# Maxima across partitions by a TensorE transpose, a VectorE maximum of the row and a one-row matmul, instead of a GpSimd reduction

## The chip, the core and the metric

The kernel runs on one core of a Trainium2 chip. The metric is the device time of one execution in microseconds (us). Engines are named as the profile names them: PE is the matmul engine (PEld its weight loads), DVE the vector engine, ACT the scalar engine, POOL GpSimd, SP the engine that issues the DMA transfers. Each engine executes its own instructions in program order, and a semaphore makes one wait for another. PSUM, where PE writes its results, is divided into banks of 2 KB in each partition; the kernel gives each result a bank of its own.

## What is computed

Banded attention over two batches of 768 tokens with eight heads, and behind it two layers of a mixture of experts over the 1536 tokens. All experts see all tokens.

```python
def _moe_ref(x, w_gate, w1, w2) -> np.ndarray:
    ...
    logits = x @ w_gate
    logits = logits - logits.max()
    P = np.exp(logits)
    for _ in range(8):
        P /= P.sum(1, keepdims=True) + 1e-09
        P /= P.sum(0, keepdims=True) + 1e-09
        P *= N / E
    out = np.zeros((N, D), dtype=np.float32)
    for e in range(E):
        h = np.maximum(x @ w1[e], 0.0)
        ye = h @ w2[e]
        out += P[:, e:e + 1] * ye
```

The first layer has eight experts; the second has four, and its weights P are given probabilities divided by their sum over the experts. `w1[e]` is 512 x 1024, `w2[e]` 1024 x 512.

## The kernel before

**Tiling.** The attention runs first (141 us of the profiled execution), then twelve experts one after the other (0 to 7 of the first layer, 8 to 11 of the second). An expert takes the tokens in three chunks of 512 (chunk 0, 1, 2). A chunk is a first product (`hidden`: 28 block products of six 128x256 matmuls each, L913, into PSUM tiles `ph`) and a second (`mixed`: 14 block products of twelve, L990, into `py`). Both are products of two by two blocks in seven instead of eight parts, and every operand is split into a high and a low float16 part, so that three matmuls make one. Between the block products DVE, ACT and POOL add blocks up (`c`, `s`), take the relu and split the results into parts (`hh` high, `hl` low) for the second product, and DVE adds `py` to the rows `acc` (L1112). A half of `hidden` covers half of the columns; its 14 block products come before those of the other half.

**Order.** The order of each engine's instructions is the order in which the program is written (`manual_schedule`). After each block product of `hidden` and each half block product of `mixed` the program calls `tick()`, which executes the small work that is due: 56 ticks a chunk, 168 an expert. The table `TICKS` says at which tick of an expert each piece of small work goes into the order; for most experts its entry "other" holds. `BALANCE` does the same for the steps of `sinkhorn` (the eight balancing iterations on `logits`, in expert 0), and `WAITS` for what follows a block product.

**The matrix scales.** Before a matrix is split into float16 parts, a power of two is found that brings its largest magnitude into range. During expert i this is done for both matrices of expert i + 1, and during the attention for expert 0: the pieces are loaded by DMA, DVE takes each piece's largest magnitude per partition (`wm`, L281) and the largest of the four (`wmm`, L290), POOL takes the largest over the 128 partitions (`wma`, L291), and DVE makes the power of two in three instructions (`pow2`, L254, L257, L259: `ws` and `wi`). In "other" the first matrix has its `wmm` and `wma` at tick 64 and `pow2` at 67, in chunk 1; the second at 120 and 123, in chunk 2. The operands of the first matrix are made from tick 111 on, those of the second in the next expert. There are 24 matrices, and `sinkhorn` has one more maximum over partitions (`mm`, L779).

**PSUM.** In the experts two pools of four banks serve all results: "ps" for those that are read only once and "pa" for the sums that several block products add to (`BANK` 0: the `ph` of products 1, 6, 7, 4, so two such tiles in each half of `hidden`), for `pt`, `pg` of the rows, and, by the same pools, for the `pc` of `sinkhorn`. A new tile takes the next bank of its pool, and PE waits until that bank's last reader is done.

Of the kernel before, what the change touches and what calls it, by code (L numbers as in the profile page):

```python
# [19 lines left out]
P = 128  # L20
GW = 32          # keys at the front that the banded attention covers as global ones
BW = P - GW      # keys before a query tile that it covers as local ones
BIG = 1.0e12
EXPONENT = 0x7F800000
# products of two by two blocks (Winograd's form of Strassen's scheme): operands of each
PRODUCTS = {1: (0, 0), 2: (1, 1), 3: (6, 2), 4: (2, 6), 5: (3, 3), 6: (4, 4), 7: (5, 5)}
BANK = {1: 0, 6: 0, 7: 0, 4: 0, 2: 1, 5: 2, 3: 2}
FIRST = (1, 2, 5)        # those that start a sum; the others add to one that has been read
ORDER1 = (1, 5, 6, 2, 7, 3, 4)
ORDER2 = (1, 5, 2, 6, 3, 7, 4)  # L30
# the quarter of the second product that a sum goes to, after each product
QUARTER = {5: (1, 1), 1: (0, 0), 6: (0, 1), 2: (0, 0), 7: (1, 1), 3: (0, 1), 4: (1, 0)}
PLACE2 = (0, 2, 3, 1, 4, 5, 6)   # where the second matrix's operands are
# the steps of the attention's even and odd units: what, and of which unit (how many before this one)
# [9 lines left out]
# The small work goes between the matrix products at numbers of ticks, counted from the start of an expert (28 for  # L44
# a chunk's product, 168 in all; during the attention: 2 a unit). Of an expert, by where it stands:
#   next1, next2: loads, largest magnitudes and scale of the next expert's first and second matrix
#   operands1: of its first matrix; for each half of the columns and each tile of the rows of a half the high and low
#     part of the first block, of the second row of blocks, the sums, the high and low part of two and of two sums
#   replace: the difference in place of its second matrix's second block
#   operands2: of its own second matrix; for each tile of the rows of a half the high and low part of the rows of  # L50
#     blocks, a sum and its parts, two sums and their parts
# "first": the first expert, -1: the last of the first layer, 0: the first of the second layer, "other": the others.
TICKS = {
    "attention": {
        "next1": ((2, 5, 7, 7), (11, 14, 13, 16), (18, 19)),
        "next2": ((11, 16, 40, 42), (22, 22, 43, 47), (49, 50)),
# [60 lines left out]
# the rows that become the second layer's operands in pairs of tiles: where the expert stands, the tile; ticks of the  # L117
# scales, the transposes, the sums, the high and low parts
# [8 lines left out]
# the same for the last rows of the attention, and their gate  # L127
KEPT = (36, 39, 44, 47, 49, 46, 48, 47, 49, 49, 50, 52, 54, 53, 55, 54, 56, 55, 60, 48, 51)
# the steps that balance the mixing weights
BALANCE = (58, 61, 58, 60, 62, 77, 80, 81, 82, 87, 87, 94, 97, 98, 98, 103, 104, 111, 114, 116, 118, 125, 122,  # L130
           143, 147, 149)
# the first expert's results: their weights, each row tile of a chunk
RESCALE = (5, 13, 14, 17, 18, 67, 79, 70, 72, 75, 121, 130, 121, 128, 127)
# ticks from a product to what follows from it, in each half of a hidden chunk
WAITS = ((0, 1, 0, 1, 0, 3, 1, 5, 3, 5, 0, 2, 7),
         (0, 1, 0, 1, 0, 1, 1, 5, 3, 5, 0, 3, 5))

# [1020 lines left out]
```

## Time and profile before

| | |
|---|---|
| times of three runs | 1735.85, 1732.91, 1747.15 us; median 1735.85 |
| the profiled execution, its span | 1735.8 us |
| busy: PE, DVE, POOL, ACT | 88 %, 76 %, 57 %, 55 % |
| mean granted TensorE clock | 0.94 of full speed |
| attention | 141 us |
| one chunk of expert 11, which prepares no next expert | 36.7 us |
| chunks 0, 1, 2 of expert 3 | 40.1, 43.1, 48.8 us |

The span of the profiled execution is the whole of its time to 0.1 us, and equals the median of the runs. A timeline row gives start and duration of an instruction, the engine, the line, output and inputs, and in brackets how long the engine had been idle before it and what released it. A row of the waits view reads: who waited for whom, total us, times, longest. Matmuls overlap: a 128x256 matmul is shown with 0.27 us, and one starts every 0.109 us at the full clock.

### The profile page before, as it was taken

Reading aid. Unit: us, or ns where it says so; the run is one execution under the profiler, and the core shown is the slowest. Engines: PE = TensorE matmul, PEld = TensorE weight load, DVE = VectorE, ACT = ScalarE, POOL = GpSimd, SP = SyncE. Lnnn points to the kernel's source line nnn. Section 1 sums busy time; section 2 is a strip of 40 time slices with the busy share of each in tenths; the row PEclk is TensorE's granted clock in tenths of the full one; section 3 lists DMA queues with packets and bytes.
Section 4 is the critical chain, followed back from the end, with each engine's and each line's share of the span. In section 5 each row is a group of like instructions: output and inputs, shape, how many; then the busy total and the mean of one; then the engine's idle time right before and its main releaser. Section 6 shows DMA issues by size and latency. Waiting matters only on the chain.

```text
span 1735.8 us, 35028 instructions
## 1 busy us (share of the span) xinstructions
PE 1532.3 (88%) x13216; PEld 1336.9 (77%) x13216; DVE 1311.4 (76%) x2903; ACT 954.7 (55%) x2515; POOL 988.2 (57%) x1274
## 2 busy tenths in 40 slices
PE   8999788888988998998998998988898898988998
PEld 7988677777877876886876886876777777777787
DVE  7897578769768757857857867877988857867855
ACT  6796536436546535535545545656665635635643
POOL 1466447448547538538537637566746735835833
PEclk9798989999998998998998999999999999999999
DMA  9520201101101101101101101100200200100011
GB/s 215 117 60 1 86 1 50 50 2 49 50 2 49 50 1 50 50 1 49 49 2 49 50 2 49 50 2 15 84 2 14 77 10 11 64 26 1 7 35 37
DMA packets 73972, 67.93 MB, mean 39 GB/s; under 512 B 52288, under 2 KB 55360, under 8 KB 73792
## 3 DMA queue, kind: packets, MB, share of 16 engines
q1 hardware_dynamic: 73792, 65.59, 13.1%
q8 instruction: 105, 1.72, 0.4%
q14 instruction: 75, 0.61, 0.1%
HBM read 62.43 MB, written 3.15 MB: 38 GB/s over the span
## 4 chain that ended last, share of the span: by engine, by line
PE 50%; POOL 21%; DVE 15%; ACT 7%; issue 7%; DMA 0%; POOLq 0%; DVEq 0%; SPq 0%; ACTq 0%
PE ph L913 27%; PE py L990 18%; POOL hl L903 14%; POOL st L305 6%; DVE w1l L298 4%; DVE w2l L298 2%; DVE acc L1112 2%; PE op L583 2%; ACT hh L903 2%; DVE s L893 1%; ACT w2h L297 1%; ACT c L945 1%; PE ep L567 1%; DVE c L893 1%; DVE xl L1051 1%
## 5 line engine op out<-in xcount | busy, mean ns | idle before, releaser
L913 PE MATMUL ph<-xh,w1h 128*128 128x256 f16 x2016 | 569.6, 283 | 110.3 <-ACT c L945 102.5
L903 POOL TENSOR_TENSOR hl<-c,hh 128x256 f16<-128x256 f32 x632 | 466.3, 765 | 246.1 <-issue 89.7
L990 PE MATMUL py<-w2h,hh 128*128 128x256 f16 x2016 | 555.1, 275 | 34.5 <-DVE acc L1112 26.6
L990 PE MATMUL py<-w2l,hh 128*128 128x256 f16 x2016 | 555.3, 275 | 26.5 <-DVE w2l L298 26.3
L913 PE MATMUL ph<-xl,w1h 128*128 128x256 f16 x2016 | 569.3, 282 | 0.0
L913 PE MATMUL ph<-xh,w1l 128*128 128x256 f16 x2016 | 568.3, 282 | 0.0
L990 PE MATMUL py<-w2h,hl 128*128 128x256 f16 x2016 | 555.5, 276 | 6.7 <-POOL hl L903 6.4
L913 PEld LDWEIGHTS <-w1h 128*128 128x128 f16 x4032 | 408.1, 101 | 176.0 <-issue 116.3
L990 PEld LDWEIGHTS <-hh 128*128 128x128 f16 x4032 | 398.3, 99 | 88.8 <-issue 39.6
L903 ACT ACTIVATE hh<-c 128x256 f16<-128x256 f32 x720 | 279.3, 416 | 117.6 <-DVE c L903 93.5
L945 ACT ACTIVATE c<-ph 128x256 f32<-128x256 f32 x432 | 158.1, 382 | 270.7 <-PE ph L913 245.7
L1112 DVE SCALAR_TENSOR_TENSOR acc<-py,mix,acc 128x256 f32<-128x256 f32 x438 | 204.5, 476 | 125.3 <-PE py L990 124.2
L990 PEld LDWEIGHTS <-hl 128*128 128x128 f16 x2016 | 199.0, 99 | 67.4 <-issue 23.4
L913 PEld LDWEIGHTS <-w1l 128*128 128x128 f16 x2016 | 204.3, 101 | 30.5
L291 POOL PARTITION_ALL_REDUCE wma<-wmm x24 | 9.1, 380 | 280.6 <-PE ph L913 140.6
L903 POOL TENSOR_TENSOR hl<-s,hh 128x256 f16<-128x256 f32 x144 | 117.4, 823 | 69.8 <-ACT hh L903 61.1
L903 DVE TENSOR_TENSOR c<-c,s 128x256 f32<-128x256 f32 x144 | 89.4, 621 | 83.0 <-POOL hl L903 83.0
L889 ACT ACTIVATE c<-c 128x256 f32<-128x256 f32 x288 | 117.3, 407 | 53.9 <-DVE c L948 45.5
L305 POOL TENSOR_TENSOR st<-raw 128x256 f32<-128x256 f32 x144 | 124.6, 875 | 16.6 <-issue 15.3
L305 POOL TENSOR_TENSOR st<-st,raw 128x256 f32<-128x256 f32 x144 | 125.3, 886 | 12.5 <-DVE w2l L298 8.7
L281 DVE TENSOR_REDUCE wm<-raw 128x1 f32<-128x1024 f32 x96 | 112.5, 1208 | 0.0
L298 DVE SCALAR_TENSOR_TENSOR w1l<-st,ws,w1h 128x512 f16<-128x512 f32 x96 | 97.4, 1014 | 15.3 <-ACT w1h L297 15.2
(157 smaller groups left out, 2000.0 us busy)
## 6 DMA issues: line engine op xcount, KB each, us to landing
raw<-in_moe_w_dram SPq DMA_DIRECT2D x96, 512.0 KB, 4.0
rows<-in_v_dram SPq DMA_DIRECT2D x12, 256.0 KB, 5.4
out_dram<-acc SPq DMA_DIRECT2D x24, 128.0 KB, 1.7
rows<-in_k_dram SPq DMA_DIRECT2D x11, 256.0 KB, 6.1
rows<-in_q_dram SPq DMA_DIRECT2D x10, 256.0 KB, 5.7
vA<-in_v_dram SPq DMA_DIRECT2D x10, 192.0 KB, 4.3
vA<-in_v_dram SPq DMA_DIRECT2D x10, 64.0 KB, 4.2
xh<-in_q_dram SPq DMA_DIRECT2D x2, 256.0 KB, 4.9
```

The lines of the kernel that those rows point to most:

```text
L281: nc.vector.tensor_reduce(out=wm[:, c:c + 1], in_=r, axis=AX.X if len(r.shape) == 2 else AX.XY, op=ALU.max, apply_absolute_value=True)
L297: return [lambda: nc.scalar.activation(hi(), src(), AF.Copy, scale=scale), lambda: nc.vector.scalar_tensor_tensor(out=lo(), in0=src(), sca ...
L298: lambda: nc.vector.scalar_tensor_tensor(out=lo(), in0=src(), scalar=scale, in1=hi(), op0=ALU.mult, op1=ALU.subtract)]
L305: nc.gpsimd.tensor_tensor(out=out, in0=a, in1=b, op=op)
L583: nc.tensor.matmul(op[:, h * D:(h + 1) * D], et[:, h, n, :], loaded[t, "v" + c][:, 4 * g + h, :], start=(n == 0), stop=(n == len(cs) - 1))
L889: nc.scalar.activation(out, src, AF.Relu)
L893: nc.vector.scalar_tensor_tensor(out=out, in0=src, scalar=0.0, in1=other, op0=ALU.max, op1=op)
L903: urgent.setdefault(state["tick"] + n, []).append(lambda: f(*args))
L913: nc.tensor.matmul(dst, a[:, wi, fs], b[:, r, :], start=(n in FIRST and m == 0), stop=(m == 3 * HC - 1), skip_group_check=n not in FIRST)
L945: nc.scalar.activation(c[p, n], src, AF.Copy)
L990: nc.tensor.matmul(src, a[:, ts], w[:, bi, :], start=(n in FIRST and k == 0), stop=(k == 3 * NH - 1), skip_group_check=n not in FIRST)
L1112: nc.vector.scalar_tensor_tensor(out=a, in0=pp, scalar=mx[:, o:o + 1], in1=a, op0=ALU.mult, op1=ALU.add)
```

## The change

Each maximum over partitions on POOL is replaced. PE transposes the column of 128 maxima into one row of PSUM (`mt`, after L290), DVE takes the maximum of that row (`top`, after L296), PE multiplies it by a row of ones, so that it stands on all 128 partitions in PSUM (`ma`, after L294), and `pow2` reads it there. A scale so has five steps instead of two, at two ticks from each other in the experts and one in the attention. `sinkhorn` gets three more steps. In the experts 1 to 11 `mt` and `ma` are tiles of the pool "pa", as in `sinkhorn`; for the matrices of expert 0 (made in the attention) of "ps". The loads of the matrices and the maxima of their pieces keep their ticks. Comments are left out in the changed file, so its line numbers differ: L903 becomes L917, L913 L927, L893 L907, L305 L315, L990 L1004, L1112 L1126.

```diff
     "other": {
-        "next1": ((2, 3, 2, 5), (57, 59, 61, 63), (64, 67)),
-        "next2": ((41, 43, 43, 42), (113, 111, 117, 118), (120, 123)),
+        "next1": ((2, 3, 2, 5), (57, 59, 61, 63), (64, 66, 68, 70, 72)),
+        "next2": ((41, 43, 43, 42), (113, 111, 117, 118), (120, 122, 124, 126, 128)),
...
-BALANCE = (58, 61, 58, 60, 62, 77, 80, 81, 82, 87, 87, 94, 97, 98, 98, 103, 104, 111, 114, 116, 118, 125, 122,
+BALANCE = (52, 54, 55, 57, 58, 60, 61, 62, 77, 80, 81, 82, 87, 87, 94, 97, 98, 98, 103, 104, 111, 114, 116, 118, 125, 122,
            143, 147, 149)
...
-    def matrix_scale(wm, s, inv, factor):
-        """steps: a matrix's power of two, on every partition"""
+    def largest_of_all(column, row, pool):
+
+        top = const.tile([1, 1], F32, tag="top", name="top", bufs=2)
+        ma = []
+
+        def across():
+            row.append(bank("mt", pool)[0:1, :P])
+            nc.tensor.transpose(row[0], column, ident)
+
+        def spread():
+            ma.append(bank("ma", pool)[:, 0:1])
+            nc.tensor.matmul(ma[0], top.to_broadcast([1, P]), ident[0:1, 0:1], start=True, stop=True)
+
+        return [across, lambda: nc.vector.tensor_reduce(out=top, in_=row[0], axis=AX.X, op=ALU.max), spread], ma
+
+    def matrix_scale(wm, s, inv, factor, pool):
+
         m = const.tile([P, 1], F32, tag="wmm", name="wmm", bufs=4)
-        ma = const.tile([P, 1], F32, tag="wma", name="wma", bufs=4)
-
-        def across():
-            nc.vector.tensor_reduce(out=m, in_=wm, axis=AX.X, op=ALU.max)
-            nc.gpsimd.partition_all_reduce(ma, m, P, bass_isa.ReduceOp.max)
-
-        return [across, lambda: all_of(pow2(s, inv, ma, factor))]
+        steps, ma = largest_of_all(m, [], pool)
+        return ([lambda: nc.vector.tensor_reduce(out=m, in_=wm, axis=AX.X, op=ALU.max)] + steps
+                + [lambda: all_of(pow2(s, inv, ma[0], factor))])
...
-        nc.gpsimd.partition_all_reduce(mm, m, P, bass_isa.ReduceOp.max)
         ones = pools["c"].tile([P, HQ], F32, tag="tq", name="ones", bufs=4)[:, :P]
         nc.gpsimd.memset(ones, 1.0)
         yield
-        nc.vector.tensor_scalar(out=mm, in0=mm, scalar1=-1.0, scalar2=None, op0=ALU.mult)
+        steps, ma = largest_of_all(m, [], "pa")
+        for f in steps:
+            f()
+            yield
+        nc.vector.tensor_scalar(out=mm, in0=ma[0], scalar1=-1.0, scalar2=None, op0=ALU.mult)
```

On POOL, in the first half of `hidden` in chunk 1 of expert 3, these rows stood before the change between the last sum of blocks of the second matrix (`st`) and the first low parts of the chunk (`hl`); an `ISA` row without names is a configuration of POOL:

```order
L305 TENSOR_TENSOR st_7756<-st_7388,raw_6136 128x256 x2
L305 TENSOR_TENSOR st_7766<-st_7402,raw_6126 128x256 x2
L291 ISA
L291 ISA wma_7322<-wmm_7321 128x1
L903 ISA
L903 TENSOR_TENSOR hl_7903<-c_7923,hh_7902 128x256
L903 TENSOR_TENSOR hl_7903<-c_7933,hh_7902 128x256
```

The same place of the changed kernel:

```order
L315 TENSOR_TENSOR st_7793<-st_7425,raw_6165 128x256 x2
L315 TENSOR_TENSOR st_7803<-st_7439,raw_6155 128x256 x2
L917 TENSOR_TENSOR hl_7940<-c_7960,hh_7939 128x256
L917 TENSOR_TENSOR hl_7940<-c_7970,hh_7939 128x256
L917 TENSOR_TENSOR hl_7946<-s_8057,hh_7945 128x256
```

The reduction and the two configurations around it are gone, and the first `hl` follows the sums of blocks directly.

On DVE, in the same half of the same chunk, the rows before the change from `pow2` to the last reader of `ph_7916`, one of the half's two sum tiles; `s` and `c` are blocks in SBUF:

```order
L254 TENSOR_SCALAR ws_7319<-wma_7322 128x1
L257 TENSOR_SCALAR ws_7319<-ws_7319 128x1
L259 TENSOR_SCALAR wi_7320<-ws_7319 128x1
L959 TENSOR_TENSOR c_7969<-ph_7944,c_7969 128x256
L903 TENSOR_TENSOR hl_7907<-c_7952,hh_7906 128x256
L893 SCALAR_TENSOR_TENSOR c_7960<-c_7960,c_7923 128x256
L893 SCALAR_TENSOR_TENSOR s_8033<-c_7969,c_7952 128x256
L893 SCALAR_TENSOR_TENSOR c_7969<-c_7969,c_7933 128x256
L903 TENSOR_TENSOR c_7923<-c_7923,s_8019 128x256
L893 SCALAR_TENSOR_TENSOR hl_7905<-ph_7916,hh_7904 128x256
L903 TENSOR_TENSOR c_7933<-c_7933,s_8033 128x256
L893 SCALAR_TENSOR_TENSOR c_7942<-ph_7916,c_7923 128x256
```

In the changed kernel, from the `s` that was `s_8033` on to `pow2`; the two sum tiles are now `ph_7953` and `ph_7962`:

```order
L907 SCALAR_TENSOR_TENSOR s_8068<-c_8006,c_7989 128x256
L296 TENSOR_REDUCE top_7359<-mt_8055 1x1
L907 SCALAR_TENSOR_TENSOR c_8006<-c_8006,c_7970 128x256
L917 TENSOR_TENSOR c_7960<-c_7960,s_8057 128x256
L907 SCALAR_TENSOR_TENSOR hl_7942<-ph_7953,hh_7941 128x256
L917 TENSOR_TENSOR c_7970<-c_7970,s_8068 128x256
L907 SCALAR_TENSOR_TENSOR c_7979<-ph_7953,c_7960 128x256
L907 SCALAR_TENSOR_TENSOR hl_7942<-ph_7962,hh_7941 128x256
L907 SCALAR_TENSOR_TENSOR c_7989<-ph_7962,c_7970 128x256
L253 TENSOR_SCALAR ws_7356<-ma_8099 128x1
```

`pow2` has moved behind the half's last four readers of its sums, and `top` stands among the work that leads to them.

On PE, the rows with waits around the new matmuls in the changed kernel; `ph_7972` is a tile of the first half, `ph_8088` and `ph_8103` are the first two of the second half, and "..." stands for the matmuls and weight loads between:

```order
L927 MATMUL ph_7972<-xh1_93,w1l_6941 128x256
L290 MATMUL mt_8055<-ident_70,wmm_7358 1x128 [waits DVE_49]
L927 LDWEIGHTS w1h_6938
...
L927 MATMUL ph_8088<-xh1_93,w1l_7201 128x256
L294 MATMUL ma_8099<-ident_70,top_7359 128x1 [waits DVE_49]
L927 LDWEIGHTS w1h_7198
L927 MATMUL ph_8103<-xh1_93,w1h_7198 128x256 [waits DVE_49]
```

Before the change the corresponding matmuls, of `ph_8052` and `ph_8065`, were without a wait:

```order
L913 MATMUL ph_7925<-xh1_93,w1l_6907 128x256
L913 LDWEIGHTS w1h_7161
L913 MATMUL ph_8052<-xh1_93,w1h_7161 128x256
...
L913 MATMUL ph_8052<-xh1_93,w1l_7164 128x256
L913 LDWEIGHTS w1h_7161
L913 MATMUL ph_8065<-xh1_93,w1h_7161 128x256
```

PE got two matmuls for each matrix, each with a wait for DVE, and the first matmul of `ph_8103`, which comes 15 block products after the chunk's first, got a wait for DVE too.

## Rows read from the trace of the kernel before

**Rows 1.** Waits over the whole span: who <- for whom, us in total, times, longest.

```profile
POOL wma L291 <- PE ph L913: 140.6, 10, 15.8
PE ph L913 <- ACT c L945: 102.5, 26, 6.7
PE py L990 <- DVE acc L1112: 26.6, 15, 3.4
```

**Rows 2.** Timeline of POOL, expert 3, chunks 1 and 2.

```profile
600.64 0.38 POOL L291 PARTITION_ALL_REDUCE wma<-wmm  x1 [12.68 <-DVE wmm L290]
607.94 1.29 POOL L903 TENSOR_TENSOR hl<-c,hh 128x256 f16<-128x256 f32 x2 [6.91 <-PE ph L913]
...
642.98 0.38 POOL L291 PARTITION_ALL_REDUCE wma<-wmm  x1 [15.56 <-PE ph L913]
650.52 1.29 POOL L903 TENSOR_TENSOR hl<-c,hh 128x256 f16<-128x256 f32 x2 [7.16 <-issue]
```

**Rows 3.** Timeline of DVE, the same stretch.

```profile
600.36 0.15 DVE L290 TENSOR_REDUCE wmm<-wm 128x1 f32<-128x4 f32 x1
...
604.70 0.42 DVE L893 SCALAR_TENSOR_TENSOR c<-c 128x256 f32<-128x256 f32 x1
608.63 0.88 DVE L903 TENSOR_TENSOR c<-c,s 128x256 f32<-128x256 f32 x1 [3.51 <-POOL hl L903]
...
642.70 0.15 DVE L290 TENSOR_REDUCE wmm<-wm 128x1 f32<-128x4 f32 x1
```

**Rows 4.** Timeline of PE, the same stretch, behind its pauses.

```profile
611.94 0.37 PE L913 MATMUL ph<-xh,w1h 128*128 128x256 f16 x1 [3.66 <-ACT c L945]
...
657.27 0.37 PE L913 MATMUL ph<-xh,w1h 128*128 128x256 f16 x1 [5.85 <-ACT c L945]
...
681.40 0.27 PE L990 MATMUL py<-w2h,hh 128*128 128x256 f16 x1 [2.15 <-DVE acc L1112]
```

**Rows 5.** Windows behind two pauses: length, busy of PE, PEld, DVE, ACT, POOL, PEclk, DMA.

```profile
610.60:617.40 6.80, 5.46 (x26) 3.78 (x26) 3.46 (x11) 5.01 (x15) 5.27 (x9) 0.50 0.00 0
682.30:685.60 3.30, 3.30 (x18) 2.38 (x16) 0.95 (x2) 1.36 (x2) 3.30 (x5) 0.50 0.33 134
```

**Rows 6.** Windows of chunk 1 of experts 1 to 10: experts 7 and 8, and the sum.

```profile
1117.83:1163.84 46.01, 40.57 (x354) 35.40 (x352) 36.36 (x86) 26.65 (x74) 22.68 (x32) 0.96 0.01 1
1259.08:1303.48 44.40, 40.28 (x355) 35.16 (x352) 36.12 (x90) 26.43 (x74) 23.24 (x33) 0.96 0.01 1
...
sum 433.30, PE 391.97 PEld 341.31 DVE 286.36 ACT 187.65 POOL 180.56; mean PE 39.20 PEld 34.13 DVE 28.64 ACT 18.76 POOL 18.06
```

**Rows 7.** Windows of chunk 2 of experts 1 to 10: their sum.

```profile
sum 483.37, PE 399.86 PEld 342.32 DVE 387.26 ACT 270.25 POOL 327.27; mean PE 39.99 PEld 34.23 DVE 38.73 ACT 27.02 POOL 32.73
```

**Rows 8.** Windows: chunk 1 of expert 0, chunk 0 of expert 3.

```profile
186.63:244.86 58.23, 42.39 (x349) 35.76 (x347) 34.12 (x99) 20.11 (x57) 20.07 (x32) 0.85 0.04 13
...
553.59:593.71 40.12, 37.32 (x339) 32.85 (x337) 32.07 (x64) 24.65 (x63) 26.46 (x33) 1.00 0.16 54
```

**Rows 9.** Chain that ended last, expert 11, chunk 1: start, us, what.

```profile
1657.43 18.34 PE ph L913 x168
1675.77 18.34 PE py L990 x168
```

**Rows 10.** Timeline of DVE, expert 11, chunk 1.

```profile
1669.24 0.41 DVE L893 SCALAR_TENSOR_TENSOR c<-ph,c 128x256 f32<-128x256 f32 x1
```

**Rows 11.** Timeline of POOL and DVE, expert 0, chunk 1, and end of the attention.

```profile
194.12 0.38 POOL L779 PARTITION_ALL_REDUCE mm<-m  x1 [5.98 <-issue]
...
215.83 0.38 POOL L291 PARTITION_ALL_REDUCE wma<-wmm  x1 [6.08 <-issue]
...
134.87 0.15 DVE L254 TENSOR_SCALAR ws<-wma 128x1 int32<-128x1 int32 x1 [2.58 <-POOL wma L291]
```

**Rows 12.** Groups by line: out<-in, count | busy us, mean ns of one | idle before.

```profile
L1023 PE MATMUL pt<-ident,acc 128*128 128x128 f32 x48 | 7.1, 275 | 0.0
L797 DVE TENSOR_REDUCE ca<-pc 128x8 f32<-128x96 f32 x8 | 2.0, 249 | 4.3 <-PE pc L794 4.3
```

More of the change, by code (lines that the diff above doesn't have):

```diff
@@ L4 @@
 import concourse.bass as bass
-import concourse.bass_isa as bass_isa
 import concourse.tile as tile
@@ L54 @@
     "attention": {
-        "next1": ((2, 5, 7, 7), (11, 14, 13, 16), (18, 19)),
-        "next2": ((11, 16, 40, 42), (22, 22, 43, 47), (49, 50)),
+        "next1": ((2, 5, 7, 7), (11, 14, 13, 16), (16, 17, 18, 19, 20)),
+        "next2": ((11, 16, 40, 42), (22, 22, 43, 47), (47, 48, 49, 50, 51)),
         "made": 14,
@@ L768, in attention_dense @@
                             f()
-                    tick(4)
+                    tick(5)
     def sinkhorn(sk, logits):
@@ L847, in weights @@
                     plan.append((t1, lambda c=c: largest(wm, c, pieces[c])))
-                return plan + list(zip(scales, matrix_scale(wm, *sc[i, second], 512.0 if second else 2.0)))
+                return plan + list(zip(scales, matrix_scale(wm, *sc[i, second], 512.0 if second else 2.0,
+                                                            "pa" if i else "ps")))
             def first_weights(i, start, at):
```

12 rows, old and new, of the table TICKS are left out of this document.

## The prediction

> **What bounds the kernel now.** I looked first at what an undisturbed chunk costs. Expert 11 prepares no next expert, and the chain that ended last runs through its chunk 1 on PE alone: 168 matmuls of the first product in 18.34 us and 168 of the second in 18.34 [rows 9], together 36.7 us at the full clock. That is the floor of a chunk as long as PE's own work stays. Then I read the windows of the chunks in which the experts 1 to 10 prepare matrices: ten chunks 1 take 433.30 us and ten chunks 2 take 483.37 [rows 6, 7], against 367.0 for ten floors. So 66.3 and 116.4 us are lost there. In chunk 1 of expert 0, in which the balancing and a matrix scale fall together, 58.23 us pass [rows 8], 21.5 over the floor. These three losses, 204 us, are what the change could touch at most in the experts; chunk 0 has no maximum over partitions, and I count nothing there.
>
> Next, who is waited for. PE's largest wait is for ACT's copy `c`: 102.5 us in 26 waits, at most 6.7 [rows 1]. ACT is only a link. On POOL the reduction takes 0.38 us, but the first `hl` behind it starts at 607.94, although the reduction was over at 601.02: 6.91 us in which POOL shows nothing. In chunk 2 it is 7.16 [rows 2]. DVE follows: its `c<-c,s` overwrites what that `hl` reads and starts 3.51 us late, at 608.63, with the instruction before it begun at 604.70 [rows 3]. DVE's lateness leaves no free `c` for ACT and no free sum tile, and PE pauses 3.66 us, in chunk 2 5.85 [rows 4]. Behind the first pause the granted clock is 0.50 for 6.8 us, which is 1.2 instead of 2.4 GHz [rows 5]; there a matmul costs double. The two, pause and half clock, make most of the lost time. In chunk 2 there is another pause of 2.15 us at the end, for DVE's `acc`, and half clock after it too [rows 4, 5]; such waits sum to 26.6 us in 15 [rows 1].
>
> POOL also stood still for 5.98 and 6.08 us before the two reductions in chunk 1 of expert 0, with nothing shown that it waited for [rows 11]. In expert 3 the same may lie hidden in the 15.56 us of idle time ahead of the reduction [rows 2]. The Trainium skill, GPSIMD Engine Reference, section 2.1 (Instruction dispatch), says that the first call of freshly loaded code pays about 6 us that no instruction shows. The trace agrees on the side before the reduction (5.98, 6.08) and adds about 7 us behind it, which that section does not name.
>
> **What the change removes.** 25 reductions with the POOL pauses around them. POOL's first `hl` of the chunk then depends on ACT's `hh` alone, DVE's `c<-c,s` is no longer late for POOL's sake, and the pause `PE <- ACT c` goes. Nothing is late on POOL next: it has been idle long before (12.68 us in expert 3 [rows 2]).
>
> **What it adds.** For each matrix PE gets a transpose of one column and a one-row matmul. The nearest rows are the fp32 transposes of 128x128 at 275 ns [rows 12]; two of them are below 0.55 us, and being pipelined they may cost next to nothing; I take 0.3 us in all, inside the wait below. DVE gets a maximum of a row of 128 in PSUM; the nearest row is a reduction of 96 columns from PSUM at 249 ns [rows 12]. 24 x 0.25 is 6 us over the whole kernel, on an engine with 28.6 of 43.3 us busy in chunk 1 and 38.7 of 48.3 in chunk 2 [rows 6, 7]. No DMA is moved: loads and maxima of the pieces keep their ticks. `pow2` is five ticks later; its results are first needed at tick 111 for the first matrix and in the next expert for the second, so that is covered, except in the attention and in expert 0.
>
> **Where a wait is added.** PE is in order, so whatever `mt`, `ma` and `ph_8103` wait for stops all matmuls behind them, and then every `c`, `acc` and `hl` that they feed. `mt` stands after 11 block products, 11 x 0.655 = 7.2 us into the chunk (0.655 is 18.34 / 28 [rows 9]). In expert 3 that is 593.71 + 7.2 = 600.9, the start being the end of chunk 0 [rows 8], and `wmm` ended at 600.51 [rows 3]: no wait, by 0.4 us. In chunk 2 it is 593.71 + 43.1 (chunk 1 in the table above) + 7.2 = 644.0 against 642.85 [rows 3]. `ma` comes after 15 products and waits for `top`, which the order of DVE puts before the sums; a few tenths.
>
> The wait that counts is the next one. `mt` and `ma` take two turns in a pool of four banks, just where the second half's two sums want theirs. `ph_8103` therefore gets the bank of `ph_7953`, whose last reader is `c_7979<-ph_7953`, one of the last rows of DVE in that half. Before the change the corresponding matmul had no wait. The undisturbed chunk shows when that reader ends: the same `c<-ph,c` runs from 1669.24 to 1669.65 [rows 10], while block product 15 is due at 1657.43 + 15 x 0.655 = 1667.26. PE thus waits 2.4 us, with `mt`, `top` and `ma` inside that. Bounds: nothing, if the banks come free some other way, and up to the old pauses (3.66, 5.85), if DVE is as late as it was. I take 2.4, since rows 10 are the very instruction, without POOL's delay. On the clock: a pause of 2.15 us was followed by 3.3 us at half speed [rows 4, 5], which costs 1.65; not every such pause need be followed by one, so I take 1.2 of 0 to 1.65.
>
> **The sum.**
> - Chunk 1, experts 1 to 6, 9, 10: 433.30 - 46.01 - 44.40 = 342.9 for eight, 49.3 over eight floors, 6.2 each. New loss 2.4 + 1.2 = 3.6. Gain 2.6 x 8 = 21. Experts 7 and 8 have 36 us of DVE work in the chunk, and their old pauses may just be replaced: 0.
> - Chunk 2, experts 1 to 10: lost 11.6 each. New loss 3.6, and at the end, where DVE with its 38.7 us of work is still behind PE's 36.7, 1.6 us (half to all of the old 2.15 and its clock). Gain 6.4 x 10 = 64.
> - Expert 0, chunk 1: of 21.5 over the floor 1.5 remain for small waits of `sinkhorn` and `pow2`. Gain 20.
> - Attention: DVE's wait of 2.58 us for `wma` [rows 11] goes, `mt` and `ma` wait for DVE a little there. Gain 2, of -4 to +4.
>
> Together 107 us. From the profiled execution's 1735.8 us, which is the median of the runs, 1629; I say 1630.
>
> **The rivals.**
> *A: the new bank wait is not there or is covered.* For it: PE waits only if DVE is behind, and DVE is freed of POOL. Against it: rows 10 come from a chunk without any POOL delay, and DVE is 2.4 us behind even there. It would give back about 3.3 us in each of 20 chunks, 66 us: 1564.
> *B: the waits take most of it back.* DVE has to do the maxima of the pieces just before, and if the bank wait grows to the old pauses of chunk 1 and to half the loss of chunk 2, 21 + 32 us of the gain go: about 1683. For it: 38.7 us of DVE work in a chunk that is to take 42.
> *C: slower.* The mechanism is the in-order PE at `mt`: it has to wait for `wmm`, which DVE reaches 0.4 us ahead of need. Each us that DVE is later than now costs 20 us in the experts. From 107 / 20 = 5.4 us on the change loses; at 7 us it is 1736 + 33 = 1769. Against it: DVE's lateness came from POOL, which is gone. The Trainium skill, GPSIMD Engine Reference, section 4.1 (Engine selection), gives reductions along the partitions to GPSIMD and speaks against leaving it; no run here shows that engine to be the better place, and rows 2 show 7 us behind 0.38 us of work.
> *D: nothing changes*, because POOL's pauses only filled idle time and PE's pauses have another source. Against it: expert 11 has no reduction and no pause. 1736.
>
> **How the numbers follow.** Forecast 0.60, A 0.18, B 0.17, C 0.02, D 0.03. A's full amount and B's are the far ends; the range 1580 to 1685 leaves out about one in ten on each side. What a measurement here can tell from no change is about 1 %, 17 us: faster 0.95, same 0.03, slower 0.02.
>
> **What would show it.** Right: no row of a POOL reduction and `hl` within 1 us of its `hh` in chunks 1 and 2; no `PE ph <- ACT c` near 6 us; in its place PE waiting for DVE at block product 15 of chunks 1 and 2, 2 to 3 us, about twenty times; chunk 1 near 40 us, chunk 2 near 42, chunk 0 still 40.1, chunk 1 of expert 0 near 38. A is shown by chunks near 37 to 38 without that wait, B by pauses of 4 us and more there or at `mt`, C by chunks longer than 43 and 49. What would make the sum wrong most: the clock, if pauses of 2.4 us are followed by half speed every time or never (24 us either way over 20 chunks), and DVE's place at the end of chunk 2.

## The result, and the profile after

The changed kernel takes 1684.13 us in the median of four runs (1681.43 to 1689.58), the kernel before 1734.43 beside it: a ratio of 0.970, with an interval of 0.966 to 0.973. It is faster by 3 %, 50 us, where the sum had 107. The direction, and the place and the mechanism of the remaining wait, came as forecast; the time lies at the far end of the range, almost exactly where rival B stood (1683). The profiled execution has 1682.4 us, 53.4 less than the one before.

First the page of the profile after: busy time by engine, and the chain that ended last by engine.

```profile
PE 1525.8 (91%) x13291; PEld 1332.1 (79%) x13291; DVE 1315.6 (78%) x2928; ACT 958.1 (57%) x2515; POOL 977.4 (58%) x1249
...
PE 49%; DVE 24%; POOL 17%; ACT 6%; issue 4%; DMA 0%; DVEq 0%; SPq 0%; POOLq 0%; ACTq 0%
```

The same chain before:

```profile
PE 50%; POOL 21%; DVE 15%; ACT 7%; issue 7%; DMA 0%; POOLq 0%; DVEq 0%; SPq 0%; ACTq 0%
```

Part of what POOL left has gone to DVE. The waits view says the same (who <- for whom: us in total, times, longest); it answers [rows 1].

```profile
PE ma L294 <- DVE top L296: 32.6, 21, 2.6
PE ph L927 <- DVE c L907: 30.0, 20, 2.8
PE py L1004 <- DVE acc L1126: 28.1, 13, 3.4
...
PE ph L927 <- ACT c L959: 4.7, 5, 1.4
```

PE's wait for ACT's copy has fallen from 102.5 us to 4.7. In its place stand two new ones that come right after each other, together 62.6 us in about twenty places, one for each scale made in the experts 1 to 10. The wait for `acc` is what it was: 26.6 before, 28.1 now.

Where the time went, from the starts of the matmuls in both traces: the attention is 4.7 us shorter, the three chunks of expert 0 together 21.2, the ten chunks 1 of the experts 1 to 10 15.0, and their ten chunks 2 12.6. That is the 53.4 us but for 0.1. The windows view has the last two, answering [rows 6, 7] (sum of the lengths; then busy times):

```profile
sum 418.26, PE 389.16 PEld 341.62 DVE 287.61 ACT 189.66 POOL 178.72; mean PE 38.92 PEld 34.16 DVE 28.76 ACT 18.97 POOL 17.87
sum 470.79, PE 405.57 PEld 344.71 DVE 391.11 ACT 270.25 POOL 316.25; mean PE 40.56 PEld 34.47 DVE 39.11 ACT 27.02 POOL 31.63
```

The first is 418 for chunk 1, against a forecast of 412; the second 471 for chunk 2, against 419. So it is chunk 2 in which the forecast gain of 64 us shrank to 13.

The timeline of PE, DVE and POOL shows one such chunk 2, in expert 3 (start, length, ..., in brackets the idle time before and its releaser). The chunk starts at 606.37, and block product 15 is due at 616.20.

```profile
618.68 0.58 PE L294 MATMUL ma<-ident,top 1*128 1x1 f32 x2 [2.21 <-DVE top L296]
620.49 0.37 PE L927 MATMUL ph<-xh,w1h 128*128 128x256 f16 x1 [1.23 <-DVE c L907]
...
611.23 0.42 DVE L962 TENSOR_TENSOR c<-ph,c 128x256 f32<-128x256 f32 x1 [0.58 <-PE ph L927]
...
614.94 0.94 DVE L907 SCALAR_TENSOR_TENSOR s<-c 128x256 f32<-128x256 f32 x1
615.81 0.41 DVE L973 TENSOR_TENSOR c<-ph,c 128x256 f32<-128x256 f32 x1
...
616.68 0.94 DVE L907 SCALAR_TENSOR_TENSOR c<-c 128x256 f32<-128x256 f32 x1
617.55 0.88 DVE L907 SCALAR_TENSOR_TENSOR s<-c 128x256 f32<-128x256 f32 x1
618.35 0.27 DVE L296 TENSOR_REDUCE top<-mt 1x1 f32<-1x128 f32 x1
...
620.03 0.41 DVE L907 SCALAR_TENSOR_TENSOR c<-ph,c 128x256 f32<-128x256 f32 x1
...
620.69 0.41 DVE L907 SCALAR_TENSOR_TENSOR c<-ph,c 128x256 f32<-128x256 f32 x1
...
612.63 1.42 POOL L917 TENSOR_TENSOR hl<-c,hh 128x256 f16<-128x256 f32 x2 [15.12 <-ACT hh L917]
614.01 0.73 POOL L315 TENSOR_TENSOR st<-raw 128x256 f32<-128x256 f32 x1
614.82 0.79 POOL L315 TENSOR_TENSOR st<-st,raw 128x256 f32<-128x256 f32 x1
615.57 0.91 POOL L315 TENSOR_TENSOR st<-raw 128x256 f32<-128x256 f32 x1
616.44 0.91 POOL L315 TENSOR_TENSOR st<-raw,st 128x256 f32<-128x256 f32 x1
617.31 0.84 POOL L917 TENSOR_TENSOR hl<-s,hh 128x256 f16<-128x256 f32 x1
```

Before, in the same chunk, with POOL standing still:

```profile
645.00 0.42 DVE L893 SCALAR_TENSOR_TENSOR s<-c 128x256 f32<-128x256 f32 x1
```

POOL is no longer late: its `hl` starts at 612.63, as soon as ACT has made `hh`. It then goes straight on to the sums `st` of the next matrix, which before came after its 7 us of standing still. But DVE's `s` and `c` take 0.88 to 0.94 us while POOL works; before, with POOL standing still, the same instructions took 0.42 (also the `c<-c` of [rows 3]). The maxima of the pieces did not make DVE late: they end at 610.64, and at 611.23 DVE has waited 0.58 us for PE. `top` is ready at 618.62 and the reader of the bank done at 620.44, and PE has lost 4.2 us. In chunk 1 the first `s` has 0.42 us and PE waits 1.15 us for `top` and 1.44 for the bank, in all 3.1 us from matmul to matmul.

### The profile page after: what moved, and what is told of

The parts are those of the page before. It is cut to its first block, busy times and chain, and to the rows that moved or that the text cites. A ratio compares the mean times of both kernels' runs of the same rounds, so it can differ in the third digit from the quotient of the medians.

```text
span 1682.4 us, 35083 instructions
## 1 busy us (share of the span) xinstructions
PE 1525.8 (91%) x13291; PEld 1332.1 (79%) x13291; DVE 1315.6 (78%) x2928; ACT 958.1 (57%) x2515; POOL 977.4 (58%) x1249
## 4 chain that ended last, share of the span: by engine, by line
PE 49%; DVE 24%; POOL 17%; ACT 6%; issue 4%; DMA 0%; DVEq 0%; SPq 0%; POOLq 0%; ACTq 0%
PE ph L927 26%; PE py L1004 19%; POOL hl L917 11%; POOL st L315 5%; DVE w1l L308 4%; DVE s L907 3%; DVE c L907 2%; ACT hh L917 2%; DVE w2l L308 2%; DVE acc L1126 2%; PE op L593 1%; DVE wm L280 1%; DVE c L973 1%; DVE xl L1065 1%; ACT c L903 1%
## 5 line engine op out<-in xcount | busy, mean ns | idle before, releaser
L917 POOL TENSOR_TENSOR hl<-c,hh 128x256 f16<-128x256 f32 x632 | 463.0, 757 | 459.0 <-ACT hh L917 430.7
L927 PE MATMUL ph<-xh,w1h 128*128 128x256 f16 x2016 | 565.1, 280 | 39.4 <-DVE c L907 30.0
L1004 PE MATMUL py<-w2h,hh 128*128 128x256 f16 x2016 | 553.2, 274 | 38.1 <-DVE acc L1126 28.1
L1004 PE MATMUL py<-w2l,hh 128*128 128x256 f16 x2016 | 553.0, 274 | 25.2 <-DVE w2l L308 25.0
L927 PE MATMUL ph<-xl,w1h 128*128 128x256 f16 x2016 | 564.5, 280 | 0.0
L927 PE MATMUL ph<-xh,w1l 128*128 128x256 f16 x2016 | 564.2, 280 | 0.0
L1004 PE MATMUL py<-w2h,hl 128*128 128x256 f16 x2016 | 553.4, 275 | 2.4 <-POOL hl L917 2.3
L927 PEld LDWEIGHTS <-w1h 128*128 128x128 f16 x4032 | 404.9, 100 | 99.1 <-issue 42.4
L1004 PEld LDWEIGHTS <-hh 128*128 128x128 f16 x4032 | 396.6, 98 | 91.6 <-issue 43.5
L1126 DVE SCALAR_TENSOR_TENSOR acc<-py,mix,acc 128x256 f32<-128x256 f32 x438 | 204.2, 476 | 121.1 <-PE py L1004 119.8
L917 ACT ACTIVATE hh<-c 128x256 f16<-128x256 f32 x720 | 276.4, 416 | 32.3 <-DVE c L907 16.4
L1004 PEld LDWEIGHTS <-hl 128*128 128x128 f16 x2016 | 198.4, 98 | 61.1 <-issue 22.8
L927 PEld LDWEIGHTS <-w1l 128*128 128x128 f16 x2016 | 202.5, 100 | 28.9
L917 POOL TENSOR_TENSOR hl<-s,hh 128x256 f16<-128x256 f32 x144 | 116.9, 814 | 118.0 <-ACT hh L917 108.3
L962 DVE TENSOR_TENSOR c<-ph,c 128x256 f32<-128x256 f32 x144 | 60.4, 421 | 120.7 <-PE ph L927 109.3
L903 ACT ACTIVATE c<-c 128x256 f32<-128x256 f32 x288 | 117.3, 407 | 50.0 <-DVE c L962 40.5
L315 POOL TENSOR_TENSOR st<-st,raw 128x256 f32<-128x256 f32 x144 | 126.6, 895 | 12.5 <-DVE w2l L308 8.7
L315 POOL TENSOR_TENSOR st<-raw 128x256 f32<-128x256 f32 x144 | 126.1, 885 | 6.0 <-PE ph L927 6.0
L307 ACT ACTIVATE w2h<-st,ws 128x256 f16<-128x256 f32 (+1 forms) x96 | 58.3, 608 | 75.2 <-POOL st L315 75.2
```

Source lines behind the costliest of these rows:

```text
L307: return [lambda: nc.scalar.activation(hi(), src(), AF.Copy, scale=scale), lambda: nc.vector.scalar_tensor_tensor(out=lo(), in0=src(), sca ...
L315: nc.gpsimd.tensor_tensor(out=out, in0=a, in1=b, op=op)
L903: nc.scalar.activation(out, src, AF.Relu)
L917: urgent.setdefault(state["tick"] + n, []).append(lambda: f(*args))
L927: nc.tensor.matmul(dst, a[:, wi, fs], b[:, r, :], start=(n in FIRST and m == 0), stop=(m == 3 * HC - 1), skip_group_check=n not in FIRST)
L962: add(a, src, a, ALU.add)
```

## The experiments

**e1: the steps in the second product of the chunk.** In the entries "other", -1 and 0, that is for the scales made in the experts 1 to 10, only `wmm` stays where it was.

```diff
     "other": {
-        "next1": (..., (64, 66, 68, 70, 72)),
-        "next2": (..., (120, 122, 124, 126, 128)),
+        "next1": (..., (64, 94, 96, 98, 100)),
+        "next2": (..., (120, 154, 156, 161, 164)),
```

> The changed kernel with the four later steps of each scale (mt, top, ma, pow2) moved out of the first product into the second product of the same chunk (entries other, -1 and 0 of the table). There mt and ma take the banks that the chunk's first product has done with, and the new sums of the next first product find their banks free. Theory (the pause is made by the two turns in the bank pool, just between two halves, with DVE in arrears): no pause at block product 15 of chunks 1 and 2, which are 3.1 and about 4.2 us in the changed kernel, nor the half clock behind most of them; the pause of 2.8 us at the end of chunk 2 stays. About 70 us of pauses and 15 to 25 of clock less: 1590 to 1605 us. Rival (DVE is behind in any case, so the pause only moves to the next matmul that waits for DVE): 1650 to 1685 us, with new rows of PE waiting for DVE in the first product.

1604.33 us (1601.4 to 1608.94), a ratio to before of 0.923 (0.919 to 0.926). The pauses at block product 15 are gone, and the waits view has no row of `ma` or of L907 among PE's larger waits:

```profile
PE py L1004 <- DVE acc L1126: 25.3, 13, 3.0
...
PE ph L927 <- ACT c L959: 10.8, 23, 1.1
...
PE ph L927 <- DVE c L967: 5.4, 6, 1.4
```

The ten chunks 1 take 383.7 us, 34.6 less than in the changed kernel, and the ten chunks 2 425.4, 45.4 less; together 80.0, which is the whole difference of the medians (79.8). The theory held: where the steps stand made the waits. Of the pause only little moved elsewhere: the wait for ACT's copy rose from 4.7 to 10.8 us, in 23 small pieces. Together with e3 and e10, from which its times can't be told, this kernel is the fastest of those that do the whole work.

**e2: `mt` and `ma` in the other pool**, same ticks, same work on DVE.

```diff
-                                                            "pa" if i else "ps")))
+                                                            "ps")))
```

> The changed kernel with mt and ma in the other pool of banks (ps), at the same places. The first matmul of the second half's second sum then has no wait for the bank; ma still waits for top. Theory (two waits make one pause: ma for top, about 1.2 us in chunk 1 and 2.2 in chunk 2, then the bank, 1.2 to 1.4): the pause shrinks to the first part, 1.2 and 2.2 us: 1682 - 20 x 1.3 = 26 us, and some of the clock: 1640 to 1660 us. Rival 1 (the bank alone counts, and ma's wait is only the same lateness seen first): pauses gone, 1600. Rival 2 (DVE's lateness passes to the next sum that takes a bank of that pool): 1675 to 1690.

1635.82 us (1634.65 to 1642.07), ratio 0.942 (0.939 to 0.946): 48 us less by a choice of bank, and 4 us under the theory's range. PE's wait for L907 is gone, the one for `top` has stayed, 32.7 us in 21. Timeline of PE, chunk 1 and chunk 2 of expert 3:

```profile
565.42 0.38 PE L294 MATMUL ma<-ident,top 1*128 1x1 f32 x2 [1.15 <-DVE top L296]
...
604.91 0.38 PE L294 MATMUL ma<-ident,top 1*128 1x1 f32 x2 [2.22 <-DVE top L296]
```

The pause is 1.6 instead of 3.1 us in chunk 1 and 2.7 instead of 4.2 in chunk 2, 30 us over twenty. The other 18 us are the clock: PE's busy time in the ten chunks 1 fell from 389.2 to 377.1 us and in the ten chunks 2 from 405.6 to 398.9, with the same matmuls. After 1.6 us, no chunk 1 of the eight ordinary experts (1 to 6, 9 and 10) had half clock behind the pause; after 3.1 us, most had. So the bank's wait sets how long the pause is, the wait for `top` alone leaves the 1.6 and 2.7 us, and less half clock follows the shorter pause.

**e3: also the maxima of the second matrix's pieces earlier**, in the second product of chunk 1.

```diff
-        "next2": (..., (113, 111, 117, 118), (120, 154, 156, 161, 164)),
+        "next2": (..., (88, 93, 98, 103), (120, 154, 156, 161, 164)),
```

> e1 with, besides, the four maxima of the pieces of the second matrix (4 x 1.2 us of DVE work) moved from the first product of chunk 2 to the second product of chunk 1, where DVE has time between the acc. Theory (the pause of 2.8 us at the end of chunk 2 is DVE in arrears by its own work of 38 us, not by POOL): that pause goes or falls below 0.5 us, in all ten chunks 2, with the half clock behind it: 30 to 45 us below e1, 1550 to 1570 us. Rival (the pause comes from the low parts w1l, which wait for ACT and POOL): as e1, within 10 us.

1605.96 us (1602.38 to 1611.09), as e1; the theory was wrong. With 4.8 us less of DVE work in the chunk, the pause at the end of chunk 2 is the same 2.5 us. The timeline, expert 3:

```profile
622.73 0.27 PE L1004 MATMUL py<-w2h,hh 128*128 128x256 f16 x1 [2.33 <-DVE acc L1126]
```

The chain that ended last leads to that `acc` by the same links in the kernel before, the changed one, e1 and e3. Before, it reads (start, us, what; chunk 2 of expert 3):

```profile
665.55 5.63 POOL hl L903 x7
671.18 1.14 POOL st L305
...
672.39 1.07 POOL st L305
...
673.48 0.73 ACT w1h L297
...
674.24 1.31 DVE w1l L298
...
678.22 1.60 DVE w1l L298 x2
...
680.22 0.74 DVE w1l L298
680.96 0.41 DVE acc L1112
```

In e3 it begins at 606.78, with 5.62, 1.14, 1.07, 0.73 and 1.31 us for the first five of these links. The `acc` that PE waits for comes at the end of a chain that begins on POOL with seven `hl` and two `st`, goes through ACT's `w1h`, and then runs over DVE's `w1l` and `acc`, with little idle time between them (from 615.46 to 622.69 in e3). The maxima of the pieces stand ahead of all this, so taking them out shortens nothing. What is excluded is the maxima, not DVE's work as a whole: its `w1l` are a part of the chain. In e10, where four `st` come later, the chain that ended last no longer goes over POOL but over DVE alone, and the `acc` comes 39.5 us into the chunk instead of 39.1: DVE's own way is about as long. What the ten chunks 2 gained elsewhere (417.7 us against 425.4 in e1) the ten chunks 1 lost (392.0 against 383.7), most of it in expert 7, which places rows there (49.3 against 43.4).

**e4: the new steps left out**, `pow2` at its new tick on each partition's own maximum.

```diff
-    return ([...wmm...] + steps + [lambda: all_of(pow2(s, inv, ma[0], factor))])
+    return ([...wmm...] + [lambda: None] * 3 + [lambda: all_of(pow2(s, inv, m, factor))])
```

> The changed kernel without mt, top and ma: pow2 reads each partition's own maximum at the same tick. It leaves out the maximum over the 128 partitions of the matrices (that of the balancing stays). It shows what all the new steps cost together where they stand: by the theory the pauses at block product 15 go with them, as in e1, and the time is that of e1 within 10 us (1590 to 1605). If it is far below e1, the new instructions cost time by themselves wherever they stand; if it stays near 1682, the pauses are not theirs.

1598.25 us (1593.78 to 1599.46), ratio 0.919 (0.915 to 0.922). The pauses at block product 15 are the new steps' and nothing else's. In seven of the eight ordinary experts a chunk 1 takes 36.7 us, the floor, against 37.2 in e1, which shows a pause of 0.40 us at `ma`: that half microsecond is what remains of the steps in a good place. The 6 us between the two medians are not their price: against e1 the ten chunks 1 are 6.3 us shorter, but the ten chunks 2 are 6.9 longer, and the attention, which scatters by as much (see e8), is 10 shorter.

**e5: the GpSimd reductions kept, but moved.** From the kernel before, the entry "other" (eight experts) alone.

```diff
-        "next1": (..., (57, 59, 61, 63), (64, 67)),
-        "next2": (..., (113, 111, 117, 118), (120, 123)),
+        "next1": (..., (57, 59, 61, 63), (97, 108)),
+        "next2": (..., (86, 89, 92, 95), (97, 109)),
```

> The kernel before, with its GpSimd reductions kept but moved, in experts 1 to 6, 9 and 10 (entry other): both matrices' maxima are finished in the second product of chunk 1, both reductions stand there at tick 97, pow2 at 108 and 109. POOL is idle there for about 15 us before the change. Theory (the old pauses came from POOL standing still ahead of work that others wait for, so the place made them, not the engine alone): the pauses of 3.7 and 5.9 us go in these eight experts, chunk 1 near 37.5, chunk 2 near 42: 8 x 11 = 90 us less, 1640 to 1660 us. Rival (POOL's 13 us of standing still hurt wherever they are, as the sums st of the next matrix are late then): 1700 us or more.

1636.52 us (1635.84 to 1638.95), ratio 0.943 (0.940 to 0.946), 3.5 us under the theory's range, with not one of the 25 reductions replaced. Timeline of POOL in chunk 1 of expert 3:

```profile
589.52 4.04 POOL L903 TENSOR_TENSOR hl<-c,hh 128x256 f16<-128x256 f32 x6
599.60 0.72 POOL L291 PARTITION_ALL_REDUCE wma<-wmm  x2 [6.04 <-DVE acc L1112]
607.44 0.71 POOL L305 TENSOR_TENSOR st<-raw 128x256 f32<-128x256 f32 x1 [7.13 <-issue]
```

The 6 us before the reductions and the 7 behind are all there, and nobody waits for POOL then: chunk 1 takes 36.7 us, the floor. Over the sixteen chunks 1 and 2 of these eight experts the kernel before needs 729.3 us, the changed one 709.9, e1 639.6 and this one 635.8. In e3, which like this one has the maxima of the second matrix's pieces in chunk 1, they take 636.3. Much the larger part of what could be won was in the place of the steps, and either engine can win it.

**e6: each matrix's reduction twice in a row**, in the kernel before.

> The kernel before with each matrix's GpSimd reduction issued twice in a row, the second writing the same values. Theory (the 7 us behind a reduction are paid for changing what POOL executes, once for each change, and the reduction itself costs 0.38 us): the second is 0.4 us long and starts at once; the 7 us stand behind the second only; time as before within 10 us (0.4 us more pause in 20 places): 1735 to 1750. Rival (each reduction pays its own 7 us): the pauses grow by 7 us in 20 places, 1860 us or more.

1749.86 us (1741.97 to 1757.97), ratio 1.008 (1.005 to 1.011), at the upper end of the theory. Timeline of POOL, expert 3:

```profile
603.36 0.38 POOL L291 PARTITION_ALL_REDUCE wma<-wmm  x1 [12.68 <-DVE wmm L290]
603.84 0.35 POOL L292 PARTITION_ALL_REDUCE wma<-wmm  x1
611.23 1.29 POOL L904 TENSOR_TENSOR hl<-c,hh 128x256 f16<-128x256 f32 x2 [7.03 <-PE ph L914]
```

The second reduction takes 0.35 us and has no 7 us of its own. The standing still belongs to the change from one sort of work to the other, and is paid once for it. The pauses of PE behind it are 4.24 and 5.91 us in this expert, 0.6 and 0.1 longer than in [rows 4], and the sixteen chunks 1 and 2 of the experts 1 to 6, 9 and 10 are 15.2 us longer together, under 1 us each, where the rival had 7.

**e7: one turn in the pool instead of two**, `ma` in the tile of `mt`.

```diff
-            row.append(bank("mt", pool)[0:1, :P])
+            both.append(bank("mt", pool))
+            row.append(both[0][0:1, :P])
...
-            ma.append(bank("ma", pool)[:, 0:1])
+            ma.append(both[0][:, P:P + 1])
```

> The changed kernel with mt and ma in one tile of the pool pa, ma in the column behind the transposed row: one turn in the pool for a scale instead of two. Theory (four banks serve two halves with two sums each; any turn between them gives the second half's second sum the bank of the first half's first sum, so one turn is as bad as two): same pauses, 1675 to 1690 us. Rival (two turns are needed for the conflict): the bank's part of the pause goes as in e2, 1630 to 1645 us.

1685.24 us (1680.73 to 1689.93), as the changed kernel; the pauses are the same 3.1 and 4.2 us. This does not compare one turn with two, though, as the times of the changed kernel in chunk 2 of expert 3 show. `ma` runs at 618.68 there. At that time three of the four banks hold sums: those of the first half have last readers to come (`c<-ph,c` at 620.03 and 620.69), and the second half's first sum has just been made. So `ma` stood in the fourth, that of `mt`, there too, and both kernels borrow one bank. One borrowed bank is enough to leave the second half's second sum the first bank of the first half.

**e8: the change in the attention, `sinkhorn` and expert 0 alone.**

> The change in the attention, in sinkhorn and in expert 0 alone; the matrices of experts 2 to 11 keep the GpSimd reduction and the old ticks. Theory (the parts add up; in the changed kernel's profile the attention is 4.7 us shorter and the three chunks of expert 0 together 21): 1708 to 1716 us. Rival (the attention's gain is a matter of the clock or of loading and does not repeat): 1716 to 1725.

1716.41 us (1710.3 to 1718.79), ratio 0.988 (0.984 to 0.992): 18 us, at the border between the theory's range and the rival's. The three chunks of expert 0 take 128.7 us, as in the changed kernel (128.3), which accounts for 21; chunk 1 is 41.3 instead of 58.2. The 4.7 us of the attention are not secured: its end lies between 131 and 141 us in the profiles of these kernels, 140.7 in e1, which has the same attention as the changed kernel with 136.4.

**e9: four `st` of the next matrix later**, in the changed kernel.

```diff
     "other": {
-                      134, 145, 143, 149, 124, 146, 149, 147, 150,
+                      134, 145, 143, 149, 134, 146, 149, 147, 150,
```

> The changed kernel with one thing moved: in experts 1 to 6, 9 and 10 the second group of POOL's sums of blocks of the next first matrix (four st of 128x256) at tick 134 instead of 124, so behind the first half's hl. In the changed kernel these st run at 614.0 to 617.3 in chunk 2 of expert 3, while DVE makes the s and c that the new bank wait needs, and those DVE rows take 0.94 us there, against 0.42 in the kernel before, where POOL stood still. Theory (DVE's instructions with two float32 inputs in SBUF take twice as long while POOL works, and that is why the pause at block product 15 is 4.2 us in chunk 2 and 3.1 in chunk 1): those rows fall to 0.42 to 0.5, the pause of chunk 2 to about 3.1; 8 x 1.1 = 9 us and perhaps some clock less, 1668 to 1676 us. Rival (the 0.94 has another source): pause 4.2 as before, 1680 to 1686.

1685.63 us (1681.69 to 1693.5), no gain. But the trace shows what the run was made for. Timeline of DVE and PE, chunk 2 of expert 3 (which starts at 602.59):

```profile
611.09 0.42 DVE L907 SCALAR_TENSOR_TENSOR s<-c 128x256 f32<-128x256 f32 x1
612.09 0.42 DVE L907 SCALAR_TENSOR_TENSOR c<-c 128x256 f32<-128x256 f32 x1
612.43 0.90 DVE L907 SCALAR_TENSOR_TENSOR s<-c 128x256 f32<-128x256 f32 x1
...
613.57 0.38 PE L294 MATMUL ma<-ident,top 1*128 1x1 f32 x2 [0.88 <-DVE top L296]
615.39 0.37 PE L927 MATMUL ph<-xh,w1h 128*128 128x256 f16 x1 [1.44 <-DVE c L907]
...
627.83 0.28 PE L1004 MATMUL py<-w2h,hl 128*128 128x256 f16 x1 [0.54 <-POOL hl L917]
```

With the `st` out of the way the two rows of 0.94 us are 0.42 again (the third has an `hl` of POOL beside it), and the pause is 2.4 to 2.9 us instead of 4.2. The mechanism stands. The forecast time does not: POOL now makes the `st` when the second half's `hl` are due, PE waits for `hl` at the start of the second product (0.7 to 1.9 us a chunk, and 0.5 more behind it), and the ten chunks 2 take 471.4 us, as before this edit (470.8).

**e10: e1 with the same four `st` later.**

> e1 with the same four st at tick 134. No pause at block product 15 is left there to shorten; the pauses of 0.4 to 0.7 us at block products 18, 21 and 33 of chunk 2 (1.7 us a chunk in e1) may shrink for the same reason. Theory: 0 to 12 us below e1, 1592 to 1604. Rival (the st come too late for their w1h and lengthen the pause of 2.5 us at the end of chunk 2): 1605 to 1625.

1603.77 us (1602.09 to 1608.78): no difference from e1 that can be measured. The small pauses at block products 18 and 21 go, and the same wait for `hl` comes in their place.

## Why the prediction was right in its direction and half wrong in its size

The range held only because it reached to rival B: the sum of the forecast was twice the measured gain.

**What the change removes: right.** No POOL reduction is left, `hl` follows `hh` at once, `PE ph <- ACT c` fell to 4.7 us, and expert 0 gave 21.2 us (17.0 in its chunk 1, where 20 were forecast, and the rest in the other two, where nothing was).

**Where a wait is added: right in place and reader, too small in size.** PE stops at block product 15 for the bank whose last reader is `c<-ph,c`, in twenty places. That it is a bank is shown by e2; which one, by the times: PE goes on at 620.49, and that reader ended at 620.44. The prediction named it rightly, though its count of two turns would have led to the next bank, whose reader ends only at 621.10: a new tile does not always take the next bank in turn (e7). Three parts of the term were too small.
- *"`ma` ... waits for `top`, which the order of DVE puts before the sums; a few tenths."* It is 32.6 us in 21, 1.15 in chunk 1 and 2.21 in chunk 2. `top` has the same tick as some of the chunk's sums, and DVE reaches it in arrears. It did not add to the 2.4 us in chunk 1 by its whole length, since both waits are for the same late engine; 3.1 came out. Nor is `top` what made the bank's wait longer: in e1, without it in that place, the reader `c<-ph,c` ends 12.94 us into chunk 1 of expert 3, and in the changed kernel 13.00. In expert 11 it was 12.38; where those 0.6 us come from stays open.
- *"I take 2.4, since rows 10 are the very instruction, without POOL's delay."* This is the step that failed. Rows 10 come from the one expert that prepares no next matrix, so from a chunk in which POOL makes no `st`. In chunk 2 of the others the four `st` that used to be held up by POOL's standing still now run beside DVE's `s` and `c`, which take 0.94 us instead of 0.42; 4.2 us came out, and e9 shows that the `st` made the difference (2.4 to 2.9 without them). The Trainium skill, GPSIMD Engine Reference, section 1 (Specifications), says that POOL's paths to SBUF are shared with VectorE and contend with DVE instructions that have two inputs in SBUF. The trace agrees: it is the rows with two SBUF inputs that double (0.94 and 0.88 against 0.42), while the `c<-ph,c` at 615.81, between them and beside an `st`, with one input in PSUM, stays at 0.41.
- *"I take 1.2 of 0 to 1.65"* for the clock. Six of the eight ordinary chunks 1 had half clock behind the pause, and two had not; at the same pause of 3.1 us that made 41.57 against 39.91 us, so 1.7. In chunk 2, with its two pauses, some 2.6 to 3.5 us of the loss are left for the clock in these experts, when the pauses are taken off.

**The end of chunk 2: wrong.** *"at the end, where DVE with its 38.7 us of work is still behind PE's 36.7, 1.6 us (half to all of the old 2.15 and its clock)"*. The pause did not shrink; it is 2.79 us in nearly all of these chunks, and the 2.15 of [rows 4] was one of the shorter before. e3 shows that taking the maxima out does not shorten it. By the trace it hangs on POOL's `hl` and `st`, by way of `w1h` and `w1l`, and the change did nothing to that way; e10 shows that DVE's own work is close behind. The forecast left a loss of 3.6 + 1.6 = 5.2 us a chunk 2; the measured one is 470.79 / 10 - 36.7 = 10.4. Of the 5.2 between them some 1.8 are the pause for the bank (4.2 instead of 2.4), 1.2 or more the pause at the end, and most of the rest the clock.

**Chunk 1** gained 15.0 us instead of 21, and 1.9 of them in the experts 7 and 8, for which nothing was counted: in the eight ordinary ones 0.7 us more pause each and, on average, a little more clock (1.7 in six of eight, where 1.2 was taken). **The attention** (2 forecast) cannot be told from its scatter.

**The rivals.** B was described as "the waits take most of it back", with 1683; the time is B's, and its mechanism nearly: not the maxima of the pieces, after which DVE was waiting for PE, but POOL's own work, freed by the change, made DVE late. A is excluded by the 30.0 us of that wait, and by e2. C did not come: `mt` waits for `wmm` nowhere near 5 us (4.1 us in 6 for all of them). Whether to leave GpSimd for this can't be settled by the changed kernel alone: e5 shows that this engine in a good place is no worse than the new steps in theirs (635.8 against 639.6 us over the same chunks in e1, and 636.3 in e3). The Trainium skill, GPSIMD Engine Reference, section 4.1 (Engine selection), gives reductions over partitions to GpSimd; it warns against VectorE for them and does not name TensorE. No run here refutes it, nor does it speak against the change.

What stays open is when a pause of some 3 us is followed by half clock and when not: the chunks 1 of experts 3 and 6 had the same 3.12 us as those of 2, 4, 5 and 9, without it, and in e7 the same pause had other experts go free.

## What to carry to other kernels

A short instruction on an engine that has to be switched over for it costs what stands still around it, so ask first whether it can stand where that engine has nothing to do: here that was worth more (e5, 98 us less than before) than replacing the engine in the old place (50 us). A replacement that borrows a buffer from a rotating pool shifts who inherits whose buffer; count the tiles that are still to be read against the buffers of the pool, and put the borrowing where one is long free (e1, 80 us less than the changed kernel). And when an engine is freed, look at what it will do in the time it gains and beside whom.

## What the runs showed of the hardware

- POOL stood still for 6.9 to 7.7 us when it went back from a reduction to tensor work, in all 25 places of the kernel before, and for 5.9 to 6.1 us ahead of the reductions whose input had been ready; two reductions in a row pay it once (0.38 and 0.35 us themselves, e6).
- DVE instructions with two float32 inputs of 128x256 in SBUF took 0.42 us with POOL at rest and up to 0.94 beside its tensor work. In the changed kernel 33 `s<-c` ran wholly beside it, with a median of 0.89 us, and 61 without any, with 0.41; 103 `c<-ph,c` of L907, with one input in PSUM, took 0.40 to 0.41 beside it.
- The maximum over partitions by way of PE and DVE costs little in a good place: `top` 0.27 us on DVE, `mt` 0.27 and `ma` 0.38 to 0.58 us on PE, and 0.5 us more for an ordinary chunk 1 (37.2 in e1, 36.7 in e4, which leaves the steps out). The fp32 one-row matmul shows as two matmul rows.
- After a PE pause of 1.6 us no ordinary chunk 1 had half clock behind it; after 3.1 us or a little more six of eight had, at about 1.7 us each.
